# Sliding-window attention feeding an MLP: a build-time scheduler with an added start order, changed load rates, and one load dependency removed

## The chip, the cores and the metric

The kernel runs on one core of a Trainium2 chip. The metric is the device time of one execution in microseconds (us). The profile's own span is some 2 us shorter than that time. Where text below compares profiled executions with each other, it compares spans or instants within them. Where it says "median", it is the device time.

A program on one core has no second die to be compared with, so the label fast or slow of a run comes from the times alone (slow: over 1.5% above the fastest run of the same kernel). Some kernels here have waits of different lengths from run to run and get the label "slow" for that reason; I therefore list their times with the mean granted clock of TensorE.

## The reference

```python
scores = (q @ k.T) / sqrt(64)            # q, k, v: 8 batches x 8 heads x 576 rows x 64, float32
mask   = 0 <= (row - col) < 64           # causal window of 64
attn   = softmax(where(mask, scores, -1e9)) @ v
x      = attn.transpose(0, 2, 1, 3).reshape(4608, 512)
h      = x @ w_in                        # 512 -> 2048
out    = (h * sigmoid(h)) @ w_out        # 2048 -> 512, float32
```

## The kernel before

The kernel does not write its instructions in program order by hand. Every piece of work is added to a `Plan`: its engine and duration, what it depends on, and for a load the transfer time. `Plan.run` then plays a list schedule on paper when the program is built, and emits the instructions of every engine in the order that came out. In the traces, what stands behind a waiting instruction on its engine waits with it: in the changed kernel DVE sat idle for 12.26 us ahead of one copy, with the masks behind it. **The plan's beliefs about durations and landings decide the order; the semaphores keep the result right whatever the beliefs are.**

How the plan believes in the landing of a load (`seen` is the time from which others may rely on it):

```python
soft = e == "POOL"
pipe[soft] = max(pipe[soft], pipe[False], end + 0.9) + op["dma"]
op["seen"] = pipe[soft] + (2.0 if c in ("xk", "xo") else 1.4)
```

The loads of q and k that GpSimd (POOL) issues, the first with a cast (`natb`), the second in rows (`nat`). Both wait in the plan for the v of the batch before (`v_landed[b - 1]`), though no data or buffer asks for it:

```python
parts[kk] += [p.add("dma", {"POOL": 0.72}, ... load_rows(i, b, pj, kk, hh),
              [nat_free.get(i)] + (v_landed[b - 1] if b > 2 else []), dma=0.6) for hh in range(2)]
...
ca = [p.add("dma", {"POOL": 0.66}, ... load_cast(w, b, pj, kk),
            [natb_free.get(w)] + (v_landed[b - 1] if b > 2 else []), dma=1.0)]
tu = p.add("turn", {"PE": us}, None, ca + [c_ident] + busy, ...)      # PE transposes what has landed
```

The v of a batch: four loads, then two copies on VectorE (DVE) that place the half-shifted rows, "the shift of v". Only then may PE multiply by v. The masks of the exponentials are on the same engine, and PE's value product of a unit (a pair of heads and a group of rows; 12 units in a batch) waits for its mask:

```python
def shift_v(b, hf, a, z):
    t = vv[b % NK][:, 2 * NB * a:2 * NB * z + 1, 0:D]
    if hf: nc.vector.tensor_copy(out=t[0:64, 2::2], in_=t[64:128, 1::2])
    else:  nc.vector.tensor_copy(out=t[64:128, 0:-1:2], in_=t[0:64, 1::2])
...
lv = v_landed[b]
sh = [p.add("shift", {"DVE": 0.1 + 0.18 * (z - a)}, ... shift_v(b, hf, a, z), lv[a:z], b=b) for hf in range(2)]
...
ma = p.add("mask", {"DVE": 0.37}, ... masking(n, g), [ex, *c_mask], b=b)
pv = p.add("pv", {"PE": 0.17}, None, [ma] + v_done[(b, pj)] + ..., lat=0.1, pool=pool, b=b)
```

At the start, warm-up matmuls fill PE's free time in the plan:

```python
nc.tensor.matmul(banks[op["bank"]][:, 0:384], lhsT=ident, rhs=bias..., start=True, stop=True)
p.add_filler(60, "warm", {"PE": 0.17}, warm, [*c_bias, c_ident], gate=...)
```

The softmax here doesn't subtract the row's maximum and nothing guards it: scores larger than these inputs give would overflow.

Of the kernel before, what the change touches and what calls it, by code (L numbers as in the profile page):

```python
# [14 lines left out]
class Plan:  # L15
# [31 lines left out]
    def run(self):  # L47
        head = {c: 0 for c in self.queues}
        engines = sorted({e for q in self.queues.values() for op in q for e in op["us"]})
        free = {e: 0.0 for e in engines}  # L50
        can = {e: [c for c, q in self.queues.items() if any(e in op["us"] for op in q)] for e in engines}
        table, left = "exp", self.count
        pipe = {True: 0.0, False: 0.0}
        events, order = [0.0], []
        while left:
            if not events:
                raise RuntimeError([(c, head[c], q[head[c]]["n"]) for c, q in self.queues.items() if head[c] < len(q)])
            now = self.now = heapq.heappop(events)
            while events and events[0] == now:
                heapq.heappop(events)  # L60
            moved = True
            while moved:
                moved = False
                for e in engines:
                    if free[e] > now:
                        continue
                    best = None
                    for c in can[e]:
                        q = self.queues[c]
                        if head[c] == len(q):  # L70
                            continue
                        op = q[head[c]]
                        if e not in op["us"] or (best and best[0]["first"] <= op["first"]):
                            continue
                        if not self.done(op["deps"]) or (op["gate"] and not op["gate"]()):
                            continue
                        if op["pool"] and not any(self.done(self.banks[i]) for i in self.pools[op["pool"]]):
                            continue
                        best = (op, c)
                    if best is None:  # L80
                        continue
                    op, c = best
                    if op["pool"]:
                        banks = self.banks
                        op["bank"] = min((i for i in self.pools[op["pool"]] if self.done(banks[i])),
                                         key=lambda i: max([u["seen"] for u in banks[i]], default=0.0))
                        banks[op["bank"]] = op["until"]
                    head[c] += 1
                    us = op["us"][e]
                    if op["table"] and op["table"] != table:  # L90
                        table, us = op["table"], us + 1.28
                    end = free[e] = now + us
                    if op["dma"] is None:
                        op["seen"] = end + op["lat"]
                    else:

                        soft = e == "POOL"
                        pipe[soft] = max(pipe[soft], pipe[False], end + 0.9) + op["dma"]
                        op["seen"] = pipe[soft] + (2.0 if c in ("xk", "xo") else 1.4)
                    op["at"], op["cls"], op["by"] = now, c, e  # L100
                    order.append((op, e))
                    left -= c != "warm"
                    moved = True
                    heapq.heappush(events, end)
                    heapq.heappush(events, op["seen"])
        for op, e in order:
            op["fn"](e)
# [3 lines left out]
def kernel(ctx, tc, q, k, v, w_in, w_out, out):  # L111
    nc = tc.nc
# [3 lines left out]
    NP = H // 2  # L116
# [3 lines left out]
    NG = 3  # L120
# [7 lines left out]
    PARTS = {0: [(0, 192), (192, TT)]}  # L128
    NXQ, NXK, NXO = 4, 2, 3
    NRAW, NOX = 2, 2  # L130
    NIV, NPM = 2, 1
    scale = 1.0 / float(D) ** 0.5

# [6 lines left out]
    ident = keep.tile([128, 128], BF16, name="ident")  # L140
# [73 lines left out]
    def clear_ob(i):  # L214
        nc.vector.memset(obs[i].bitcast(FP32), 0.0)

    c_ident = p.add("one", {"POOL": 0.5}, const_ident)
    c_vv = [p.add("one", {"DVE": 0.25}, lambda _, i=i: clear_vv(i)) for i in range(NK)]
    c_k = [p.add("one", {"DVE": 0.15}, lambda _, i=i: clear_k(i)) for i in range(NK)]
    c_zero = p.add("one", {"DVE": 0.1}, lambda _: nc.vector.memset(zero, 0.0))  # L220
# [37 lines left out]
    def load_v(e, b, part):  # L258
        g0, g1 = part * 9, part * 9 + 9
        queue[e].dma_start(  # L260
            out=vv[b % NK][:, 2 * g0 + 1:2 * g1 + 1:2, 0:D],
            in_=v[b].rearrange("h s d -> (h s) d").rearrange("(g p) d -> p g d", p=128)[:, g0:g1],
        )

    def load_w_in(f):
        nc.gpsimd.dma_start(
            out=w_in_sb[:, :, f * 256:(f + 1) * 256],
            in_=w_in[:, f * 256:(f + 1) * 256].rearrange("(c p) f -> p c f", p=128),
        )

    def load_w_out(f):
        nc.gpsimd.dma_start(
            out=w_out_sb[:, 2 * f:2 * f + 2, :],
            in_=w_out[f * 256:(f + 1) * 256, :].rearrange("(c p) m -> p c m", p=128),
        )
# [174 lines left out]
    win, wout = [], []  # L450
# [21 lines left out]
    def add_batch_qk(b):  # L472
        pool = "at" if b else "all"
        slot, parts = {}, {0: [], 1: []}
        for pj in range(NP):
            kq_done[(b, pj)] = []
            busy = s_last.get((b - NK, pj), []) + ([c_k[b % NK]] if b < NK else [])
            for kk in range(2):
                if b >= (NXK if kk else NXQ):
                    if pj % 2 == 0:  # L480
                        slot[kk] = n_nat[0] % NN
                        n_nat[0] += 1
                    i = slot[kk]
                    parts[kk] += [p.add("dma", {"POOL": 0.72}, lambda _, i=i, pj=pj, kk=kk, hh=hh: load_rows(i, b, pj, kk, hh),
                                        [nat_free.get(i)] + (v_landed[b - 1] if b > 2 else []), dma=0.6) for hh in range(2)]
                    if pj % 2 == 0:
                        continue
                    both = busy + s_last.get((b - NK, pj - 1), [])
                    if kk:
                        done = [p.add("xk", {"SP": 1.4}, lambda _, i=i, pj=pj: turn_rows(i, k_place(b, pj - 1)),  # L490
                                      parts[kk] + both, dma=2.9)]
                        nat_free[i] = done[0]
                    else:
                        w = n_raw[0] % NRAW
                        n_raw[0] += 1
                        x = p.add("xk", {"SP": 1.4}, lambda _, i=i, w=w: turn_rows(i, raws[w].rearrange("x j s -> x (j s)")),
                                  parts[kk] + raw_free.get(w, []), dma=2.9)
                        nat_free[i] = x
                        done = [p.add("spread", {"DVE": 0.5}, lambda e, w=w, pj=pj, hh=hh: spread_q(e, w, b, pj - 1, hh),
                                      [x] + both, b=b) for hh in range(2)]  # L500
                        raw_free[w] = done
                    parts[kk] = []
                    for x in (pj - 1, pj):
                        kq_done[(b, x)] += done
                    continue
                w = n_nat[1] % NNB
                n_nat[1] += 1
                ca = [p.add("dma", {"POOL": 0.66}, lambda _, w=w, pj=pj, kk=kk: load_cast(w, b, pj, kk),
                            [natb_free.get(w)] + (v_landed[b - 1] if b > 2 else []), dma=1.0)]
                by = {"ACT": 0.64, "DVE": 0.75}  # L510
                li = []

# [20 lines left out]

    def add_v_loads(b, parts, busy):
        v_landed.setdefault(b, []).extend(
            p.add("dma", {"POOL": 1.0}, lambda e, part=part: load_v(e, b, part), busy, dma=1.3) for part in parts)

    def add_batch_v(b):
        busy = pv_last.get(b - NK, []) + [c_vv[b % NK]]
# [9 lines left out]
    def add_batch_attention(b):  # L549
        pv_last[b], o_rows = [], []  # L550
        pool = "at" if b else "all"
        for g, pj in [(g, pj) for pj in range(NP) for g in range(NG)] if b < NPM else [(g, pj) for g in range(NG) for pj in range(NP)]:
                n = len(g_pv)
                s = p.add("s", {"PE": 0.17 if b else 0.4}, None,
                          kq_done[(b, pj)] + g_pv[n - NE:n - NE + 1] * (n >= NE) + ([] if b else c_bias) + c_q.get(b, []),
# [98 lines left out]


    def warm(op):
        nc.tensor.matmul(banks[op["bank"]][:, 0:384], lhsT=ident, rhs=bias.rearrange("k x h i -> k (x h i)"),  # L657
                         start=True, stop=True)

    p.add_filler(60, "warm", {"PE": 0.17}, warm, [*c_bias, c_ident], gate=lambda: moe[40][0]["seen"] is None,  # L660
                 pool="all")
    for f in range(8):
        win.append(p.add("dma", {"POOL": 0.8}, lambda _, f=f: load_w_in(f), dma=1.55))
    add_batch_attention(0)
    n_tile = 0
    for b in range(1, B):
        add_batch_qk(b)
        add_batch_v(b)
        if b == 1:
            for f in range(8):  # L670
                wout.append(p.add("dma", {"POOL": 0.8}, lambda _, f=f: load_w_out(f), dma=1.38))
        while TB * (n_tile + 1) <= b * NB:
            add_tile(n_tile)
            n_tile += 1
        add_batch_attention(b)
# [34 lines left out]
```

## Time and profile before

| kernel before | value |
|---|---|
| median time | 317.98 us (4 runs, 317.68 to 318.04) |
| span of the profiled execution | 315.6 us |
| TensorE (PE) busy | 97% |
| mean granted TensorE clock | 1.0 |
| first MLP matmul starts | 24.80 us |
| first value product of batch 6 starts | 182.70 us |
| last matmul ends | 312.31 us |

The prediction below shows the page's busy table, PE's waits and the turns of batch 3's q (a turn is a transpose on PE), and reads them. The first value product of batch 6, from which the account further down counts, is this line of PE's timeline (start, busy time, engine, line of the program, operation, tiles and count):

```profile
182.70 0.34 PE L363 MATMUL at<-vv,e 128*128 128x130 bf16 x3
```

One view it doesn't show also belongs here. This is the timeline of DVE in the kernel before, with the same columns; in brackets is the idle time before it and what ended it:

```profile
182.09 0.74 DVE L358 TENSOR_TENSOR e<-e,mask 128x384 bf16<-128x384 bf16 x2 [0.33 <-ACT e L355]
...
197.93 0.76 DVE L325 COPY vv<-vv 64x2304 bf16<-64x2304 bf16 x1
...
199.36 0.75 DVE L323 COPY vv<-vv 64x2304 bf16<-64x2304 bf16 x1
```

The first masks of batch 6 run at 182.09. The two copies that shift batch 7's v come 16 us later. The last of that v had landed at 188.35 (from the issue and landing of its four loads in the trace), so the copies waited for nothing.

### The profile page before, as it was taken

Reading aid. Unit: us, or ns where it says so; the run is one execution under the profiler, and the core shown is the slowest. Engines: PE = TensorE matmul, PEld = TensorE weight load, DVE = VectorE, ACT = ScalarE, POOL = GpSimd, SP = SyncE. Lnnn points to the kernel's source line nnn. Section 1 sums busy time; section 2 is a strip of 40 time slices with the busy share of each in tenths; the row PEclk is TensorE's granted clock in tenths of the full one; section 3 lists DMA queues with packets and bytes.
Section 4 is the critical chain, followed back from the end, with each engine's and each line's share of the span. In section 5 each row is a group of like instructions: output and inputs, shape, how many; then the busy total and the mean of one; then the engine's idle time right before and its main releaser. Section 6 shows DMA issues by size and latency. Waiting matters only on the chain.

```text
span 315.6 us, 6086 instructions
## 1 busy us (share of the span) xinstructions
PE 307.6 (97%) x2231; PEld 167.7 (53%) x2231; DVE 152.8 (48%) x465; ACT 194.1 (61%) x381; POOL 120.8 (38%) x161
## 2 busy tenths in 40 slices
PE   5899999999999999999999999999999999999995
PEld 2668666545655456545654565455444444444444
DVE  5691858854788638895895089606800000000000
ACT  8798795787848687467618762777176136316611
POOL 8965958876748642867645400000000000000000
PEclk9999999999999999999999999999999999999999
DMA  7999999999999999999999995302320110020011
GB/s 68 173 194 189 158 200 167 154 226 160 144 152 158 152 95 159 200 162 132 157 162 188 167 156 119 83 1 56 95 58 2 66 66 2 18 82 33 3 66 66
DMA packets 137309, 37.03 MB, mean 117 GB/s; under 512 B 121664, under 2 KB 132800, under 8 KB 137280
## 3 DMA queue, kind: packets, MB, share of 16 engines
q0 software_dynamic: 96128, 18.36, 78.6%
q1 hardware_dynamic: 41152, 18.29, 31.1%
q8 instruction: 17, 0.28, 0.4%
q14 instruction: 12, 0.10, 0.1%
HBM read 36.70 MB, written 9.44 MB: 146 GB/s over the span
## 4 chain that ended last, share of the span: by engine, by line
PE 92%; DVE 2%; DMA 2%; ACT 1%; POOL 1%; issue 1%; POOLq 0%; ACTq 0%; DVEq 0%
PE mp L428 39%; PE mp L437 39%; PE at L363 5%; PE at L337 5%; DMA natb<-in_q_dram 2%; PE at L296 1%; PE at L419 1%; PE at L287 1%; PE at L657 0%; DVE qbd L309 0%; POOL natb L232 0%; PE mp L657 0%; ACT L355 0%; PE mp L408 0%; POOL vv L260 0%
## 5 line engine op out<-in xcount | busy, mean ns | idle before, releaser
L437 PE MATMUL mp<-w_out_sb,g 128*128 128x512 bf16 (+2 forms) x608 | 145.4, 367 | 0.0
L428 PE MATMUL mp<-bridge,w_in_sb 128*128 128x512 bf16 (+2 forms) x640 | 129.7, 358 | 0.1
L434 ACT ACTIVATE g<-mp 128x512 bf16<-128x512 f32 (+2 forms) x160 | 86.5, 555 | 30.0 <-PE mp L428 29.7
L428 PEld LDWEIGHTS <-w_in_sb 128*128 128x128 bf16 x640 | 60.4, 98 | 59.6 <-issue 0.4
L437 PEld LDWEIGHTS <-g 128*128 128x128 bf16 x608 | 54.4, 97 | 41.3
L443 ACT COPY ot<-mp 128x512 f32<-128x512 f32 (+2 forms) x36 | 20.1, 563 | 73.7 <-PE mp L437 56.8
L392 DVE TENSOR_TENSOR ox<-at,rc 64x192 bf16<-64x192 f32 x120 | 42.4, 354 | 2.6
L242 POOL DMA_DIRECT2D nat<-in_k_dram x48 | 36.1, 754 | 17.1 <-DMA vv<-in_v_dram 7.0
L260 POOL DMA_DIRECT2D vv<-in_v_dram x32 | 32.0, 1002 | 24.8 <-PE at L363 15.5
L355 ACT ACTIVATE e<-at 128x384 bf16<-128x384 f32 x89 | 37.9, 498 | 2.1 <-PE at L337 1.9
L358 DVE TENSOR_TENSOR e<-e,mask 128x384 bf16<-128x384 bf16 x84 | 26.5, 346 | 24.5 <-ACT e L355 23.8
L363 PEld LDWEIGHTS <-e 128*128 128x128 bf16 x288 | 22.6, 96 | 15.2 <-DVE e L358 2.1
L363 PE MATMUL at<-vv,e 128*128 128x130 bf16 x273 | 29.8, 219 | 0.0
L242 POOL DMA_DIRECT2D nat<-in_q_dram x32 | 24.3, 764 | 7.9 <-DMA nat<-in_q_dram 4.7
L337 PE MATMUL at<-qbd,kt 128*128 128x128 bf16 x252 | 22.8, 219 | 0.2
L337 PEld LDWEIGHTS <-kt 128*128 128x128 bf16 x252 | 17.8, 98 | 9.6 <-issue 1.4
L369 DVE RECIPROCAL rc<-at 128x6 f32<-128x6 f32 x91 | 17.3, 194 | 10.0 <-PE at L363 8.2
L302 DVE COPY qbd<-at 64x288 bf16<-64x288 bf16 x25 | 12.0, 479 | 16.0 <-ACT qbd L302 14.4
L375 DVE TENSOR_TENSOR ob<-at,rc 64x192 bf16<-64x192 f32 x48 | 16.8, 350 | 0.9
L256 DVE COPY qbd<-raw 64x1152 bf16<-64x1152 bf16 x16 | 7.9, 497 | 13.2 <-DMA raw<-nat 12.9
L302 ACT COPY qbd<-at 64x288 bf16<-64x288 bf16 x23 | 11.0, 478 | 2.9 <-DVE qbd L302 1.9
L232 POOL DMA_DIRECT2D natb<-in_q_dram x16 | 10.7, 670 | 4.8 <-PE mp L428 1.3
(66 smaller groups left out, 160.9 us busy)
## 6 DMA issues: line engine op xcount, KB each, us to landing
out_dram<-ot SPq DMA_DIRECT2D x35, 256.0 KB, 2.5
vv<-in_v_dram POOLq DMA_DIRECT2D x32, 144.0 KB, 6.9
nat<-in_k_dram POOLq DMA_DIRECT2D x48, 72.0 KB, 8.0
natb<-in_q_dram POOLq DMA_DIRECT2D x16, 144.0 KB, 6.3
nat<-in_q_dram POOLq DMA_DIRECT2D x32, 72.0 KB, 8.1
w_in_sb<-in_moe_w_in_dram POOLq DMA_DIRECT2D x8, 256.0 KB, 8.4
w_out_sb<-in_moe_w_out_dram POOLq DMA_DIRECT2D x8, 256.0 KB, 8.3
natb<-in_k_dram POOLq DMA_DIRECT2D x8, 144.0 KB, 5.9
```

Source lines behind the costliest of these rows:

```text
L242: nc.gpsimd.dma_start(out=rows(i)[:, pj % 2, :, 64 * hh:64 * hh + 64], in_=(q, k)[kk][b, 2 * pj + hh].rearrange("(m p) d -> p m d", p=NR),)
L260: queue[e].dma_start(out=vv[b % NK][:, 2 * g0 + 1:2 * g1 + 1:2, 0:D], in_=v[b].rearrange("h s d -> (h s) d").rearrange("(g p) d -> p g d", ...
L302: copies[e](out=qbd[b % NK][64 * hh:64 * hh + 64, pj, hh].rearrange("x (p m) -> x p m", m=NM)[:, :, r::2], in_=at_bf16(op)[64 * r:64 * r + ...
L337: nc.tensor.matmul(at_sp(op)[:, x], lhsT=kt[b % NK][:, pj * S + t * 64:pj * S + t * 64 + 128], rhs=qbd[b % NK][:, pj, :, t * 64:t * 64 + 6 ...
L355: nc.scalar.activation(out=es[n % NE], in_=at_sp(op), func=ACTF.Exp, scale=scale)
L358: nc.vector.tensor_mul(es[n % NE], es[n % NE], mask0 if g == 0 else mask)
L363: nc.tensor.matmul(at_pv(op)[:, x], lhsT=es[n % NE][:, x].rearrange("p h i -> p (h i)"), rhs=vv[b % NK][:, s:s + NB + 1:NB, 0:D + 1], star ...
L392: nc.vector.tensor_mul(ox(n)[:, :, r], pv[r, :, hh, 0:D], rc[r, :, hh:hh + 1].to_broadcast([64, 3, 64]))
L428: nc.tensor.matmul(banks[bank["bank"]][:, lo:hi], lhsT=w_in_sb[:, c, ft * 128:(ft + 1) * 128], rhs=bridge[:, (j * TT + lo) // 64:(j * TT + ...
L434: nc.scalar.activation(out=gts[gt][:, lo:hi], in_=banks[bank["bank"]][:, lo:hi], func=ACTF.Silu)
L437: nc.tensor.matmul(banks[bank["bank"]][:, 0:hi - lo], lhsT=gts[gt][:, m * 128:(m + 1) * 128], rhs=w_out_sb[:, f, lo:hi], start=(f == 0), s ...
L443: copies[e](out=ots[ot][:, lo:hi], in_=banks[bank["bank"]][:, 0:hi - lo])
```

## The change

By its diff it alters what the plan believes: loads are faster, loads after 60 us land up to 3 us later, and loads of q and k no longer depend on the older v, so that their landings may be planned earlier. Beside that, batch 0's units get an order of their own, and the warm-ups no longer wait for `bias`. The diff of the program (`...` marks what is left out; the last two changes stand on one line each):

```diff
-  op["seen"] = pipe[soft] + (2.0 if c in ("xk", "xo") else 1.4)
+  op["seen"] = pipe[soft] + (2.0 if c in ("xk", "xo") else 1.4) + ({"xo": 1.0}.get(c, 3.0) if now > 60 else 0.0)
...
+  UNITS0 = [(0, 0), (1, 0), (2, 0), (0, 1), (1, 1), (2, 1), (0, 2), (1, 2), (0, 3), (2, 2), (1, 3), (2, 3)]
...
-  c_ident = p.add("one", {"POOL": 0.5}, const_ident)
+  c_ident = p.add("one", {"POOL": 1.3}, const_ident)
...
-      [nat_free.get(i)] + (v_landed[b - 1] if b > 2 else []), dma=0.6) for hh in range(2)]
+      [nat_free.get(i)], dma=0.6) for hh in range(2)]
...
-      [natb_free.get(w)] + (v_landed[b - 1] if b > 2 else []), dma=1.0)]
+      [natb_free.get(w)], dma=0.85 if b else 1.0)]
...
-      p.add("dma", {"POOL": 1.0}, lambda e, part=part: load_v(e, b, part), busy, dma=1.3) for part in parts)
+      p.add("dma", {"POOL": 1.0}, lambda e, part=part: load_v(e, b, part), busy, dma=1.1 if b else 1.3) for part in parts)
...
-  for g, pj in [(g, pj) for pj in range(NP) for g in range(NG)] if b < NPM else ...
+  for g, pj in UNITS0 if b < NPM else ...
...
-  nc.tensor.matmul(banks[op["bank"]][:, 0:384], lhsT=ident, rhs=bias.rearrange("k x h i -> k (x h i)"),
+  nc.tensor.matmul(banks[op["bank"]][:, 0:384], lhsT=ident, rhs=ident.unsqueeze(1).to_broadcast([128, 3, 128]),
-  p.add_filler(60, "warm", {"PE": 0.17}, warm, [*c_bias, c_ident], ...)
+  p.add_filler(60, "warm", {"PE": 0.17}, warm, [c_ident], ...)
...
-  load_w_in(f), dma=1.55        ->  +  load_w_in(f), dma=1.35
-  load_w_out(f), dma=1.38       ->  +  load_w_out(f), dma=1.28
```

Lines of the program move by 2: what is L296 before is L298 after, and so on.

More of the change, by code (lines that the diff above doesn't have):

```diff
@@ L551, in add_batch_attention @@
         pool = "at" if b else "all"
-        for g, pj in [(g, pj) for pj in range(NP) for g in range(NG)] if b < NPM else [(g, pj) for g in range(NG) for pj in range(NP)]:
+        for g, pj in UNITS0 if b < NPM else [(g, pj) for g in range(NG) for pj in range(NP)]:
                 n = len(g_pv)
@@ L656, in warm @@
     def warm(op):
-        nc.tensor.matmul(banks[op["bank"]][:, 0:384], lhsT=ident, rhs=bias.rearrange("k x h i -> k (x h i)"),
+        nc.tensor.matmul(banks[op["bank"]][:, 0:384], lhsT=ident, rhs=ident.unsqueeze(1).to_broadcast([128, 3, 128]),
                          start=True, stop=True)
-    p.add_filler(60, "warm", {"PE": 0.17}, warm, [*c_bias, c_ident], gate=lambda: moe[40][0]["seen"] is None,
+    p.add_filler(60, "warm", {"PE": 0.17}, warm, [c_ident], gate=lambda: moe[40][0]["seen"] is None,
                  pool="all")
     for f in range(8):
-        win.append(p.add("dma", {"POOL": 0.8}, lambda _, f=f: load_w_in(f), dma=1.55))
+        win.append(p.add("dma", {"POOL": 0.8}, lambda _, f=f: load_w_in(f), dma=1.35))
     add_batch_attention(0)
@@ L670 @@
             for f in range(8):
-                wout.append(p.add("dma", {"POOL": 0.8}, lambda _, f=f: load_w_out(f), dma=1.38))
+                wout.append(p.add("dma", {"POOL": 0.8}, lambda _, f=f: load_w_out(f), dma=1.28))
         while TB * (n_tile + 1) <= b * NB:
```

## The prediction

> **What bounds the kernel now.** The page's busy table and its 40 slices came first.
>
> ```profile
> PE 307.6 (97%) x2231; PEld 167.7 (53%) x2231; DVE 152.8 (48%) x465; ACT 194.1 (61%) x381; POOL 120.8 (38%) x161
> ...
> PE   5899999999999999999999999999999999999995
> ...
> DMA  7999999999999999999999995302320110020011
> ```
>
> TensorE (PE) is full from the third slice on, and the DMA engines are full for the first 24 slices (about 190 us). The list of PE's waits says how much of PE's time is waiting:
>
> ```profile
> PE at L657 <- DVE bias L191: 3.5, 1, 3.5
> PE at L287 <- DMA natb<-in_q_dram: 0.6, 1, 0.6
> PE mp L408 <- DVE ox L398: 0.2, 1, 0.2
> ```
>
> The only long one is the very first: the warm-up matmuls wait for `bias`. The chain of waits ends with the two MLP layers alone (13.8 us per layer of a tile). I then added up PE's own work from the first MLP matmul, at 24.80 us in the timeline, by start-to-start times from the trace: first layer 64 x 0.083 + 64 x 0.1365 + 512 x 0.2158 = 124.5; second layer 560 x 0.2158 + 16 x 0.109 + 32 x 0.056 = 124.4; scores 252 x 0.056 = 14.1; values 252 x 0.058 = 14.6; turns of q, k and o some 7.5; five warm-ups 0.8. Sum 286.0. PE's last matmul ends at 312.31, so 287.5 us passed: **all stalls after 24.80 come to 1.5 us**. No reordering can win more than that plus what it takes off the first 24.8 us.
>
> [...]one matmul that waits for a load holds up everything behind it; the 0.6 us wait above is an example. [...]warm-ups start 0.32 us apart from 3.53 us and 0.16 us apart by 7 us. [...]while SyncE's queue carries transposes or stores, GpSimd's loads slow down (below).
>
> **The change, part by part.** Counting both built programs, every matmul of the work is there in the same number; only warm-ups rise, from 35 to 51. The rest is order.
>
> 1. *The unit order of batch 0.* It swaps just two units: (group 0, pair 3) goes ahead of (group 2, pair 2). The number and kinds of PE instructions before the first MLP matmul are the same, still with all batch-0 units ahead, so this gains nothing I can see: 0.
>
> 2. *The first microseconds.* `ident` is now planned at 1.3 us, which puts the three GpSimd steps of `window` ahead of the first q load. In the timeline they take 2.28 to 3.09, so the first load starts about 0.8 later, at 2.3 instead of 1.49; the second starts where it did (3.09). Warm-ups now need `ident` alone, which is ready at 1.31, and there are 27 before the first q turn. Some 8 or 9 at 0.32 (cold) and 18 at 0.162 make 2.8 + 2.9, so the first turn comes near 7.2 instead of 6.45. But PE idled until 10.31 for the second q:
>
> ```profile
> 10.31 0.56 PE L287 MATMUL at<-ident,natb 96*64 96x96 bf16 x12 [0.59 <-DMA natb<-in_q_dram]
> ```
>
> That wait swallows nearly all of it. The second q may land 0 to 0.4 later[...]. I put +0.2 on the start of the MLP (25.0).
>
> 3. *Batch-1 turns earlier, 25 to 43 us.* They stand up to 3 us earlier in PE's order. Walking the new order with the durations above, they come at 29.84, 30.77, 32.60 ... 38.90; the loads landed at 29.34, 30.02, 31.78 ... 37.53 before. They fit, by 0.5 us or more. The late lifts that held the first batch-1 scores (0.46 us of stall around 43) should go.
>
> 4. *Batch-3 q turns earlier: the part that decides.* Before, the plan held batch-3 loads back until batch-2's v had landed. The built GpSimd order, apart from the swap in part 2, is unchanged, so the loads go out as before; only PE's plan now believes in an earlier landing. Before, these turns stood at:
>
> ```profile
> 73.12 0.42 PE L296 MATMUL at<-ident,natb 96*128 96x96 bf16 x6
> 75.32 0.42 PE L296 MATMUL at<-ident,natb 96*128 96x96 bf16 x6
> 77.53 0.42 PE L296 MATMUL at<-ident,natb 96*128 96x96 bf16 x6
> 95.31 0.42 PE L296 MATMUL at<-ident,natb 96*128 96x96 bf16 x6
> ```
>
> In the new order the first stands directly ahead of the second MLP tile, and 9, 8 and 8 first-layer matmuls separate the four. My walk gives 63.1, 65.3, 67.2, 69.2, plus a few tenths of stalls before it. When do the loads land? The timeline of GpSimd gives their issue, and the DMA view narrowed to each gives the time to landing (8.6, 7.9, 6.4, 6.3 us):
>
> ```profile
> 56.88 0.68 POOL L232 DMA_DIRECT2D natb<-in_q_dram  x1
> ...
> 59.00 0.65 POOL L232 DMA_DIRECT2D natb<-in_q_dram  x1
> ...
> 61.77 0.64 POOL L232 DMA_DIRECT2D natb<-in_q_dram  x1 [0.18 <-issue]
> ...
> 65.73 0.73 POOL L242 DMA_DIRECT2D nat<-in_k_dram  x1 [1.54 <-DMA natb<-in_q_dram]
> 66.60 0.64 POOL L232 DMA_DIRECT2D natb<-in_q_dram  x1
> ```
>
> That is 65.5, 66.9, 68.2 and 72.9; the fourth line confirms the first, for GpSimd itself waited for that load until 65.7. All four land after PE wants them. The first is late because four v loads and a k transpose on SyncE's queue stand in front of it; the fourth because of four 256 KB stores issued from 63.8 on. So PE stalls from about 63.5 to 65.5. The first MLP matmul of tile 1, at 63.84 before, then comes at 65.5 + 0.25 = 65.75; less the 0.25 of turn work already done, the lag is 1.65. The second turn comes at 65.75 + 9 x 0.216 = 67.7 (landed), the third at 67.7 + 0.25 + 8 x 0.216 = 69.65 (landed), the fourth at 71.6: it waits until 72.9, **1.3 more**. Sum 2.95.
>
> 5. *A second late landing, hidden by the first.* VectorE now does batch 3's shift of v (two copies of 0.75) ahead of batch 2's first masks. The last of that v landed at 81.3, so masks cannot start before 82.8 (before: 81.12). With PE already 2.9 late, the masks come at about 84 anyway: 0 more. Alone it would cost about 1.7.
>
> 6. *Later.* Parts of batch-3 and batch-4 attention move up to 17 us earlier (94 to 137 us), with kt landed by 85 and v by 81. From about 147 us the two orders walk to the same microsecond. Nothing there can win the lag back, since PE has no idle time to give. Of the small stalls after 64 us (0.7 in all) perhaps 0.2 go.
>
> Sum: +2.95 - 0.2 = +2.75. The +0.2 at the start and the saved 0.46 at 43 do not count, as the stall ends at a landing, not after a count of work. 317.97 + 2.75 = 320.7. I shade it to **320.2**, because a change that was kept may have been kept for a measured gain, and a load can land earlier than my trace says.
>
> **Rivals.**
> *(a) The loads land in time.* If the earlier turns or the removed wait let the loads go out earlier, nothing stalls: PE does its 286.0 from 25.0, stalls shrink to 0.5 to 1, and the time is 316.5 to 317.5. For it: the removed wait was meant for that. Against it: GpSimd's order is the same, and its issues between 40 and 70 us wait for older loads, not for PE; the DMA engines are full.
> *(b) The start decides.* If warm-ups without `bias` or the unit swap brought the MLP forward, it would start up to 1 us sooner, 317. Against it: the first q's turn was never what the start waited for, and the new warm-ups make it later.
> *(c) Stalls compound.* [...]if the loads land 1 to 2 us later than before, it could cost 2 to 4 more: 323 to 325.
>
> **Range and chances.** Six parts in ten for my sum, three for (a) or half of the stall, one for more: 80% between 317.0 and 322.1. Two per cent is 6.4 us. Faster by that is impossible with 1.5 us of stalls and a start bound by loads (1%); slower needs (c) (3%).
>
> **What the new profile would show.** PE's waits with a line of the q turns (now L298) on a DMA into natb, 2 us near 65 and 1.3 near 72; the PE slice at 63 to 72 below nine; the first MLP matmul of tile 1 near 65.7; scores of batch 2 near 81.5 instead of 78.6; the last layer starting near 301.2 instead of 298.4; first MLP matmul near 25.0. I am wrong if the batch-3 q turns run at 63 to 70 without a wait, or if the first MLP matmul moves by more than 0.5 us.

## The result and the profile after

The changed kernel takes **329.33 us** (median of 4 runs: 327.81, 327.82, 330.84, 331.47), against 317.98. The ratio is 1.0364, with a 95% interval of 1.0288 to 1.0439: slower. Such a ratio is the mean time of one kernel's fast runs over that of the other's of the same rounds, so not quite the ratio of the medians. The prediction was 320.2, with at most 322.1.

The busy table and the slices of the page after:

```profile
PE 313.5 (96%) x2247; PEld 170.5 (52%) x2247; DVE 156.1 (48%) x468; ACT 193.4 (59%) x378; POOL 120.2 (37%) x161
...
PE   8999999878999999999999969999999999999995
...
PEclk9999999999999999999999969999999999999999
```

PE has two dips, at slices 8 to 10 (57 to 82 us) and in slice 24 (187 to 196 us), where the granted clock falls too. PE's busy time grew by 5.9 us: 3.1 of them ahead of the first MLP matmul, where warm-ups were added (20.45 us busy before, 23.57 after), and the rest at the second dip, since matmuls at a lower clock count as longer (a 128x512 one 623 ns in the mean from 190.4 to 196 us, 378 from 196.5 to 210). The list of PE's waits (total, how often, longest):

```profile
PE at L298 <- DMA natb<-in_q_dram: 3.8, 2, 2.4
PE at L365 <- DVE e L360: 3.3, 1, 3.3
PE at L659 <- POOL ident L180: 1.4, 1, 1.4
```

The first is the predicted wait of batch 3's q turns. The second was not predicted: a value product waits 3.3 us for a mask. PE's timeline at both places:

```profile
65.49 0.43 PE L298 MATMUL at<-ident,natb 96*128 96x96 bf16 x6 [1.46 <-DMA natb<-in_q_dram]
...
67.70 0.42 PE L298 MATMUL at<-ident,natb 96*128 96x96 bf16 x6
...
69.69 0.42 PE L298 MATMUL at<-ident,natb 96*128 96x96 bf16 x6
...
74.20 0.43 PE L298 MATMUL at<-ident,natb 96*128 96x96 bf16 x6 [2.37 <-DMA natb<-in_q_dram]
...
190.42 0.51 PE L365 MATMUL at<-vv,e 128*128 128x130 bf16 x3 [3.33 <-DVE e L360]
```

Why was the mask late? DVE's timeline after, which answers to the one shown of before:

```profile
187.51 0.76 DVE L327 COPY vv<-vv 64x2304 bf16<-64x2304 bf16 x1 [12.26 <-DMA vv<-in_v_dram]
188.28 0.76 DVE L325 COPY vv<-vv 64x2304 bf16<-64x2304 bf16 x1
189.05 0.92 DVE L258 COPY qbd<-raw 64x1152 bf16<-64x1152 bf16 x2
190.01 0.63 DVE L360 TENSOR_TENSOR e<-e,mask 128x384 bf16<-128x384 bf16 x2
```

**The shift of batch 7's v now stands ahead of every mask of batch 6.** Counted in the traces, 60 of the 84 masks run before it, where it was 74 before. DVE sits idle for 12.26 us for a v that batch 6 has no use for, then works off the copies, and only then makes the mask that PE stands still for. The plan had put the shift at 177.9 us, when it believed that v to be there; its last load landed at 187.40. The load itself came no later than in the kernel before (188.35): what changed is what stands behind it.

The view by stretches adds the clock. Its columns are the stretch, its length, busy us (and instructions) of PE, weight loads, DVE, ACT and POOL, then the granted clock, DMA share and GB/s:

```profile
186.90:189.00 2.10, 0.19 (x1) 0.00 (x0) 1.47 (x2) 0.91 (x3) 0.00 (x0) 1.00 1.21 229
189.00:189.50 0.50, 0.00 (x0) 0.00 (x0) 0.49 (x2) 0.00 (x0) 0.00 (x0) 0.75 0.00 0
189.50:196.00 6.50, 5.58 (x27) 3.26 (x28) 4.50 (x17) 1.95 (x4) 0.00 (x0) 0.50 0.07 26
196.00:196.50 0.50, 0.50 (x8) 0.37 (x7) 0.34 (x2) 0.00 (x0) 0.00 (x0) 0.92 0.50 184
```

During the wait the clock halves, near 189.25, and it stays halved until about 196.08, long after PE is back at work at 190.42.

**The account of the profiled executions.** Batch 6's first value product started at 182.70 before and at 190.42 after: 7.72 us later. From there to the end of the last matmul it is 129.61 us before (312.31 - 182.70) and 132.36 after (322.78 - 190.42): 2.75 more, the halved clock. The sum, 10.47, is the whole difference of the last matmul. The later start (25.66 against 24.80) and the waits at the q turns are inside the 7.72: batch 6's scores, just ahead, start 4.22 us late (183.62 against 179.40), and the other 3.50 come with the wait for the mask. PE could have been at that point 3.5 us sooner, but the mask would not have been.

### The profile page after: what moved, and what is told of

Its sections match the earlier page's. It is cut to its first block, busy times and chain, and to the rows that moved or that the text cites. A ratio compares the mean times of both kernels' runs of the same rounds, so it can differ in the third digit from the quotient of the medians.

```text
span 326.1 us, 6119 instructions
## 1 busy us (share of the span) xinstructions
PE 313.5 (96%) x2247; PEld 170.5 (52%) x2247; DVE 156.1 (48%) x468; ACT 193.4 (59%) x378; POOL 120.2 (37%) x161
## 4 chain that ended last, share of the span: by engine, by line
PE 63%; DMA 20%; POOL 7%; issue 7%; DVE 2%; ACT 1%; POOLq 0%; DVEq 0%; ACTq 0%
PE mp L439 26%; PE mp L430 24%; DMA vv<-in_v_dram 7%; DMA natb<-in_q_dram 5%; DMA nat<-in_k_dram 5%; POOL nat L244 4%; DMA nat<-in_q_dram 3%; POOL vv L262 3%; PE at L365 3%; PE at L339 3%; PE at L659 2%; PE mp L659 1%; PE at L289 1%; PE at L410 0%; PE at L298 0%
## 5 line engine op out<-in xcount | busy, mean ns | idle before, releaser
L439 PE MATMUL mp<-w_out_sb,g 128*128 128x512 bf16 (+2 forms) x608 | 147.3, 371 | 0.0
L439 PEld LDWEIGHTS <-g 128*128 128x128 bf16 x608 | 55.1, 98 | 42.4 <-issue 0.3
L357 ACT ACTIVATE e<-at 128x384 bf16<-128x384 f32 x91 | 39.1, 497 | 9.7 <-PE at L339 6.3
L244 POOL DMA_DIRECT2D nat<-in_q_dram x32 | 23.6, 748 | 7.1 <-DMA vv<-in_v_dram 3.8
L304 DVE COPY qbd<-at 64x288 bf16<-64x288 bf16 x28 | 13.4, 478 | 13.3 <-ACT qbd L304 7.4
L327 DVE COPY vv<-vv 64x576 bf16<-64x576 bf16 (+1 forms) x14 | 8.8, 629 | 13.0 <-DMA vv<-in_v_dram 12.7
L426 ACT CAST bridge<-at 128x192 bf16<-128x192 f32 x24 | 7.6, 320 | 5.2 <-PE at L421 4.0
```

What stands on the lines that cost most here:

```text
L244: nc.gpsimd.dma_start(out=rows(i)[:, pj % 2, :, 64 * hh:64 * hh + 64], in_=(q, k)[kk][b, 2 * pj + hh].rearrange("(m p) d -> p m d", p=NR),)
L357: nc.scalar.activation(out=es[n % NE], in_=at_sp(op), func=ACTF.Exp, scale=scale)
L439: nc.tensor.matmul(banks[bank["bank"]][:, 0:hi - lo], lhsT=gts[gt][:, m * 128:(m + 1) * 128], rhs=w_out_sb[:, f, lo:hi], start=(f == 0), s ...
```

## The experiments

Eight kernels were run, in two jobs of four with three rounds each. Every one gave correct results. Before, in the rounds of the first job: 317.59 us (23 runs); in those of the second: 317.31 us (23 runs).

**Theory.** The loss comes from the places that too early a belief in landings gives to instructions that wait for a load: above all the shift of batch 7's v on DVE, then the q turns of batch 3 on PE. **Rival 1:** the loss is at the q turns (the prediction's own mechanism, only larger). **Rival 2:** loads that go out at other times crowd the transfers and slow everything. **Rival 3:** the new start or unit order costs the time.

The view by which the experiments are compared is the same as in the account above:

| kernel | batch 6's first value product, us | last matmul ends, us | between, us | median time, us |
|---|---|---|---|---|
| before | 182.70 | 312.31 | 129.61 | 317.98 |
| changed | 190.42 | 322.78 | 132.36 | 329.33 |
| x_shift | 183.97 | 313.57 | 129.60 | 320.29 |
| x_turn | 189.72 | 321.00 | 131.28 | 325.24 |
| x_fill | 189.68 | 319.29 | 129.61 | 326.81 |
| x_fill2 | 190.16 | 319.79 | 129.63 | 323.93 |
| x_dep | 182.97 | 312.57 | 129.60 | 317.71 |
| x_all | 182.03 | 311.64 | 129.61 | 317.44 |
| x_best | 180.53 | 310.15 | 129.62 | 315.29 |

Once past that point, every kernel whose clock stays full needs the same 129.6 us. (x_b_dep is left out: its wait lies in batch 5.) In the three traces in which PE waits for this mask, the product comes the same 3.02 to 3.03 us after the last landing of batch 7's v: 187.40 and 190.42 in the changed kernel, 186.69 and 189.72 in x_turn, 187.13 and 190.16 in x_fill2.

### x_shift: batch 7's v alone believed later

```diff
-  op["seen"] = pipe[soft] + ...
+  op["seen"] = pipe[soft] + ... + op.get("slip", 0.0)
   lv = v_landed[b]
+  for x in lv:
+      x["slip"] = {7: 14.0}.get(b, 0.0)
```

> The changed kernel, whose plan is told that batch 7's v lands 14 us later, and nothing else: its two shift copies on VectorE then stand behind batch 6's masks again. Theory (the stall at 187 us is VectorE waiting in order for batch 7's v, and the half clock behind it follows from that stall): both go, 3.5 + 2.7 us, so about 322 us; the two waits of the batch-3 q turns (1.6 and 2.5) stay. Rival (PE only meets the next late load a little later): less than 2 us gained, 326 or more.

Measured: 320.29 us (318.65, 320.00, 320.58, 321.04), ratio 1.0099 (1.0074 to 1.0123), a verdict of "same" at the 2% line, though clear of 1. Mended alone, the place of two copies on an engine that is half idle leaves 2.7 us (320.29 - 317.59) of the 11.35 (329.33 - 317.98), each against the kernel before of its own rounds. PE's list of waits in this run:

```profile
PE at L661 <- POOL ident L180: 1.4, 1, 1.4
PE at L410 <- DVE ox L400: 0.6, 1, 0.6
PE at L298 <- DMA natb<-in_q_dram: 0.5, 1, 0.5
```

The wait for the mask is gone and so is the halved clock (mean 1.0 in the profiled run). The q turns waited only 0.5 us in this execution, where they waited 3.8 in the changed kernel's: the landings differ from run to run. So the expectation that both waits stay was not met in the profiled run. Rival 1 falls, since the q turns stand where the change put them and all four runs lose 3.5 us or less.

### x_turn: batch 3's q turns alone believed later

```diff
   ca = [p.add("dma", ... load_cast(w, b, pj, kk), [natb_free.get(w)], dma=0.85 if b else 1.0)]
+  ca[0]["slip"] = 7.0 if b == 3 else 0.0
```

> The changed kernel, whose plan is told that batch 3's q loads land 7 us later: the four turns move some 7 us back in PE's order, all else stays. The two waits of 1.6 and 2.5 us must go. Theory (every wait ends at a landing that does not depend on PE): PE then arrives earlier at batch 3's v (shift done near 82.6) and at batch 7's v (187), waits longer there, and the time falls by 0 to 2 us, to 326 to 328. Rival (the waits add up): it falls by the full 4.2 us, to about 324.

Measured: 320.56, 324.43, 326.04 and 329.13 us, with mean clocks of 0.999, 0.993, 0.993 and 0.984; ratio of those labelled fast 1.0160 (1.0085 to 1.0235), a verdict of "unclear". The profile (of the 326.04 run) says what became of the time:

```profile
PE at L365 <- DVE e L360: 4.9, 1, 4.9
PE at L660 <- POOL ident L180: 1.4, 1, 1.4
PE at L339 <- DVE qbd L304: 1.1, 1, 1.1
```

The waits at the q turns are gone, PE comes earlier to the mask and stands there for 4.9 us in place of 3.3. The product starts at 189.72, just 0.70 earlier than in the changed kernel, and v had landed 0.71 earlier. **In this trace, what PE wins ahead of an instruction that waits for a landing is given back there.** The rest of the 1.78 us between the two profiled executions (326.04 and 327.82) is the clock, halved here for 3.41 us and not 6.83. The medians do not decide between theory and rival: 325.24 lies below the theory's 326 to 328 and above the rival's 324, and the runs lie on both sides. The third line is a copy of q that stands on DVE behind the two copies of batch 3's v shift (which waited for v until 80.97 us); that shift the prediction had put at 1.7 us if nothing hid it, and it costs 1.1 here. The spread shows more than the theory expected: in the 320.56 run the mask may have come earlier, but that run left no trace.

### x_fill: dummy matmuls where PE waits for the mask

```diff
+  if b == 6 and g == 0 and pj == 0:
+      def filled(...):
+          for _i in range(12):
+              nc.tensor.matmul(banks[pv["bank"]][:, 0:384], lhsT=ident, rhs=ident..., start=True, stop=True)
+          values(pv, n, 6, pj, g)
+      pv["fn"] = filled
```

> The changed kernel with 12 warm-up matmuls (about 2 us) ahead of the first value product of batch 6, where PE stands idle for 3.3 us. Theory (the half clock of 190.4 to 196 us comes from PE's own idleness): the clock stays full and some 2.7 us go, about 325 us, while the wait itself ends at the same 190.4. Rival (the half clock comes from something else, power or the state of the chip): the granted clock still falls to 0.5 there and the time is 328 or more.

Measured: 324.80, 326.02, 327.61 and 330.22 us, clocks 0.999, 0.994, 0.995 and 0.988; ratio 1.0275 (1.0231 to 1.0320). In the profile the clock stays full at 190 and the rest takes 129.61 us. But this execution did not test the filling. PE's and DVE's timelines:

```profile
187.73 2.11 PE L573 MATMUL at<-ident 128*128 128x384 bf16 x12
189.68 0.34 PE L365 MATMUL at<-vv,e 128*128 128x130 bf16 x3
```

```profile
187.25 0.63 DVE L360 TENSOR_TENSOR e<-e,mask 128x384 bf16<-128x384 bf16 x2
```

Batch 7's v had landed at 184.63, PE came late (at 187.73), and the mask that its product needs was begun at 187.25; by the 0.41 us from mask to product in the changed kernel (190.01 and 190.42) it was ready at about 187.66. PE had nothing to wait for, and the dummies cost the 1.95 us until 189.68. That the 2.75 us of the account are the halved clock rests on the table: 129.60 to 129.63 us in every kernel with a full clock there, 132.36 with 5.66 us at half clock (190.42 to 196.08), 131.28 in x_turn with 3.41. Half of these two times is 2.83 and 1.71, against 2.75 and 1.67 measured. In this run the clock halved elsewhere, after the wait at the last q turn (PE idle from 71.1 to 73.3):

```profile
71.10:73.30 2.20, 0.00 (x0) 0.00 (x0) 0.95 (x2) 0.47 (x1) 1.50 (x3) 1.00 1.60 169
74.00:74.50 0.50, 0.50 (x3) 0.19 (x2) 0.00 (x0) 0.01 (x1) 0.50 (x1) 0.85 1.60 158
74.50:77.50 3.00, 3.00 (x8) 1.06 (x7) 0.95 (x2) 1.66 (x3) 1.85 (x4) 0.50 2.65 150
77.50:78.00 0.50, 0.50 (x3) 0.25 (x2) 0.00 (x0) 0.18 (x1) 0.50 (x1) 0.73 2.41 153
```

In the changed kernel's own profile an idle time of 2.37 us at the same place had left the clock full (1.00 from 74 to 78 us); why was not shown. (This run also ended 1.7 us later after its last matmul than the others, 4.97 us against 3.3 in most; I did not find out why.)

### x_fill2: dummies at both places

```diff
   # x_fill, and:
+  if b == 3 and pj == 3 and twos:
+      def turn_filled(...):
+          for _i in range(10):
+              nc.tensor.matmul(banks[tu["bank"]][:, 0:384], lhsT=ident, rhs=ident..., start=True, stop=True)
+          turn_twos(tu, w)
```

> The changed kernel with dummy matmuls at both long waits: 12 ahead of batch 6's first value product as in the earlier run, and 10 (1.6 us) ahead of batch 3's last q turn. The results stay right. Theory (the spread of 324.8 to 330.2 us of the earlier run, and of 327.8 to 331.5 us of the changed kernel, is the clock halved or not halved after a long wait): mean granted clock 0.997 or more in every run, 323.5 to 326 us, all runs within 2 us. Rival (the spread comes from the landings, that is from the waits themselves): the same spread and median as with one filling, about 326.8 us.

Measured: 321.96, 322.86, 325.00 and 329.03 us, clocks 1.0, 1.0, 1.0 and 0.995; ratio 1.0176 (1.0127 to 1.0224), a verdict of "unclear". Three of four runs keep the full clock, as expected, and the median is 6.6 us over the kernel before of its rounds (323.93 - 317.31), where x_fill's was 9.2 (326.81 - 317.59); for the runs labelled fast alone it is 5.6 and 8.4. But they are not within 2 us of each other, and one still lost clock: the expectation fails in that. So both seem true: part of the spread is the clock, and the 3.0 us between the runs at full clock (321.96 to 325.00) must come from elsewhere, most likely the landings; this was not traced. In its profile PE came to the mask at 185.0 us, did 2.1 us of dummies, waited 3.06 us more and went on at 190.16, with the clock full. This is the run that tests the filling.

### x_dep: the removed dependency restored, the rest of the change kept

```diff
-  [nat_free.get(i)], dma=0.6)
+  [nat_free.get(i)] + (v_landed[b - 1] if b > 2 else []), dma=0.6)
-  [natb_free.get(w)], dma=0.85 if b else 1.0)
+  [natb_free.get(w)] + (v_landed[b - 1] if b > 2 else []), dma=0.85 if b else 1.0)
```

> The changed kernel with one part undone: the loads of q and k are again planned behind the older v. The turns and both shifts then stand late again. Theory (the removed dependency is what causes all the waits): no wait of PE over 0.5 us after the first MLP matmul, full clock, only the later start (+0.9) remains: 318 to 319.5. Rival (the new rates and the late landings have a share): over 321.

Measured: 317.71 us (20 runs, 316.69 to 319.10), ratio 1.0002 (0.9986 to 1.0017). PE's list of waits has one line left, the start. That is just under the expected 318 to 319.5: the first MLP matmul is 0.78 us later than before, but the last one ends only 0.26 later. **The loss hangs on the removed dependency; the unit order, the rates, the late term and the start together are worth nothing either way, once it is back.** Rival 3 falls.

### x_b_dep: the removed dependency alone, on the kernel before

```diff
   # the diff of x_dep the other way round, in the kernel before
```

> The kernel before with one part of the change alone: no load waits for an older v. Its plan puts batch 7's v shift after 62 masks (two units into batch 6) and batch 3's q turns at 68.7 to 75.3 us of the plan, 5 us later than the changed kernel. Theory: no wait over 1 us at the q turns, and a wait of 3 to 5 us at batch 6's third value product for a mask behind the shift; 320 to 325 us, over 322 if the clock halves after the wait. Rival (the removal does harm only together with the new rates and the late term): 317.5 to 318.5 us.

Measured: 326.21 us (325.03 to 326.79, clock 0.989 in every run), ratio 1.0263 (1.0235 to 1.0292). Slower as expected (though above the expected 320 to 325) and with no wait at the q turns, but **the place was not the one expected**, and the wait was 7.27 us, not 3 to 5. PE's and DVE's timelines:

```profile
158.06 0.51 PE L365 MATMUL at<-vv,e 128*128 128x130 bf16 x3 [7.27 <-DVE e L360]
```

```profile
156.86 0.75 DVE L327 COPY vv<-vv 64x2304 bf16<-64x2304 bf16 x1 [5.68 <-DMA vv<-in_v_dram]
157.64 0.90 DVE L360 TENSOR_TENSOR e<-e,mask 128x384 bf16<-128x384 bf16 x3
```

Here it is the shift of batch **6**'s v that stands ahead of batch 5's masks. This plan put it at 149.8 us; the load landed at 156.74. Batch 7's shift, which I had named, waited for 1.66 us and held up nothing. So one part alone gives the same fault in another batch: with the dependency gone, which shift goes wrong is a matter of small numbers. I had looked for the wait where the changed kernel has it and not walked the whole order of DVE a second time.

### x_all: the dependency stays removed, three landings believed later

```diff
+  ca[0]["slip"] = 7.0 if b == 3 else 0.0                       # q loads of batch 3
+  x["slip"] = {3: 10.0, 7: 14.0}.get(b, 0.0)                   # v loads of batches 3 and 7
```

> The changed kernel with the dependency still removed, but the plan is told that three loads are ready later than it assumed: batch 3's q loads by 7 us, batch 3's v by 10 us, batch 7's v by 14 us. Nothing else is touched. Theory (the loss is only the place that wrong beliefs about landings give to the q turns and to the v shift in the engines' orders): none of the waits over 1 us is left, and the time is that of the version with the dependency restored, 317.3 to 318.7 us. Rival (loads that go out earlier crowd the transfers and slow other engines, whatever the order): still 320 us or more, with waits elsewhere.

Measured: 317.44 us (20 runs, 316.68 to 318.71), ratio 1.0006 (0.9995 to 1.0017), and no wait of PE but the start. The whole loss is gone with the dependency still removed. And in all ten traces, this one and x_dep's included, GpSimd's 152 loads come in the same order: with or without the dependency, no load was moved. Only the order of instructions on the other engines differs. Rival 2 falls, and this run with x_dep settles the cause.

### x_best: the dependency restored and fewer warm-ups

```diff
   # x_dep, and:
-  p.add_filler(60, "warm", {"PE": 0.17}, warm, [c_ident], ...)
+  p.add_filler(60, "warm", {"PE": 0.26}, warm, [c_ident], ...)
```

> A better version: the changed kernel with the dependency restored, and a warm-up matmul planned at 0.26 us in place of 0.17, so that 18 in place of 27 warm-ups stand ahead of the first turn. 11 cold ones of 0.32 and 7 of 0.16 from 1.36 us on end at 6.0 us, where the version with the dependency restored began its first turn at 8.1 us, with that load landed at 5.5 us. If the start is on the path that sets the end, up to 1.2 us are won: 316.3 to 317.3 us. If the later start was hidden behind other waits of the first batch: 317.7 us as before.

Measured: **315.29 us** (315.10 to 315.45), ratio 0.9924 (0.9903 to 0.9945): faster than both kernels, by 0.8% against the kernel before (a verdict of "same" at the 2% line, but all four runs lie below the fastest of the 23 before, 316.64), and by more than the expectation's 316.3. Its start in PE's timeline:

```profile
6.01 0.56 PE L289 MATMUL at<-ident,natb 96*64 96x96 bf16 x12
...
9.37 0.32 PE L289 MATMUL at<-ident,natb 96*64 96x96 bf16 x3 [0.74 <-DMA natb<-in_q_dram]
```

The first turn runs at 6.01, where the estimate had 6.0 and x_dep 8.1. The estimate counted the nine warm-ups fewer ahead of the first turn; in the traces 18 fewer stand ahead of the first MLP matmul (28 against 46 in x_dep). That matmul starts at 22.59 us against 24.80 before, and those 2.2 us are still there at the last matmul (310.15 against 312.31).

## Why the prediction was wrong

- **The step that failed is part 6, "Later": "From about 147 us the two orders walk to the same microsecond. Nothing there can win the lag back".** The walk followed PE's order alone, and from there to batch 6's first value product that order is indeed the same. DVE's order was not walked. Part 5 even described this very fault for batch 3 (the shift of v ahead of the masks of the batch before), and rightly found it hidden there; the same move of batch 7's shift was overlooked. Step 6 had -0.2; the runs show a wait for the mask that adds 3.50 us to PE's lag of 4.22, and then 2.75 for the clock: 10.47 at the last matmul, where the sum had 2.75. Of the 7.72 that are missing, 6.25 belong to this step and 1.47 to the lag (part 4). The view that would have shown it existed beforehand: which instructions stand ahead of which on DVE, beside the trace's landing of batch 7's v at 188.35.
- **Part 4 had the mechanism right and the size too small.** The turn at 65.5 came at 65.49, but that exactness was luck: in the other eight traces, of kernels with the same order of loads, the same load landed between 62.25 and 64.97. The turn at 72.9 came at 74.20, as the load landed at 74.16, 1.3 us later than in the kernel before. The lag behind the q turns was 4.46 us (first scores of batch 2 at 82.89, before at 78.43), not 2.95. In x_turn's trace this cost did not add up with the wait behind it.
- **Two of the prediction's own signs** were met badly: the last layer starts at 308.88, not near 301.2, and the first MLP matmul moved by 0.86, over the 0.5 at which it called itself wrong.
- **Part 5 was right**: nothing extra in the changed kernel; without the q turns' waits, 1.1 us in x_turn.
- **Parts 1 and 3 were right** as far as they go: no gap over 0.25 us is left near 43 us, and x_dep shows the sum of all parts but the dependency to be zero.
- **Part 2 was too small**: +0.2 predicted. In the seven profiled kernels with this start order the first MLP matmul came at 24.40, 24.94, 25.45, 25.58, 25.66, 26.09 and 26.19, a mean of 25.47, so +0.7 with a spread of nearly 2 us. I had counted 8 or 9 cold warm-ups; in the changed kernel there are 11 (0.32 us apart), so the first turn came at 7.59, not 7.2. And the start was taken to be bound by loads. But in the changed kernel the second q landed at 8.88 (10.27 before) and its turn still came only at 10.47: PE was behind with its own queue. In x_best the same start with fewer warm-ups wins time, so PE's start is on the path, which the case against rival (b) had denied.
- **Rival (c)** looked for the added cost at the q turns; the 2 to 4 us that it gives for later landings were shown by no trace. The clock halved in a wait of 3.33 us at another place, and in x_fill after 2.23 us at the q turn. The chance of 3% for slower was too low for a prediction that had found one belief to be too early and had not asked which other instructions rest on such beliefs.
- **GpSimd's loads beside SyncE's transfers:** that they slow down, the prediction says without a rate. In the half-microseconds of the trace before, from 30 to 190 us, GpSimd's queue moved 146 GB/s on average where SyncE's queue carried nothing (its packets' time under 1% of 16 engines' time), and 44 GB/s where that share was 50 to 100%. By what mechanism was not shown.

**What stays open:** which of the plan's shifts goes wrong depends on small differences (batch 7 in the changed kernel, batch 6 in x_b_dep), and why the two slowest runs of the changed kernel, 330.84 and 331.47 us, took 3 us longer was not traced; their mean clocks of 0.984 and 0.983 against 0.988 and 0.989 fit a longer time at half clock. That the removed dependency served as a stand-in for the program's limit on outstanding loads (last section) is an argument, not shown. Why x_turn's fastest run took only 320.56 us was not traced either.

## What to carry to other kernels

In a static schedule, walk the order of **every** engine, not only of the one that bounds the kernel (here a copy on DVE waited for 12.26 us and the masks behind it with it), and ask of each instruction that waits for a transfer what stands behind it and who waits for that. A belief in a landing that is 7 to 14 us later cost nothing here (x_all); one that is too early puts a wait in front of ready work (3.33 us of PE in the changed kernel, 7.27 in x_b_dep). Such waits need not add up along the engine: in the three traces with the wait for the mask, the last landing set its end. But they can cost clock on top: it was halved for 6.83 us in the changed kernel and 3.41 in x_turn, and stayed full in x_fill2.

## What else the traces show

- The clock and the length of PE's waits. The clock was halved in or after waits of 2.23 us (x_fill: for 3.41 us, 74.35 to 77.77), 3.33 us (changed kernel: for 6.83 us, 189.25 to 196.08), 4.9 us (x_turn: for 3.41 us) and 7.27 us (x_b_dep: 0.50 from 155 to 161 us). It stayed full after waits of 2.37 us (changed kernel, 74.20) and 3.06 us (x_fill2). So the length of the wait alone does not decide; what does was not shown.
- GpSimd's loads in flight. Of the 144 loads after the first eight, in each of the traces of the kernel before, the changed one and x_b_dep, none finished issuing earlier than 0.99 us after the landing of the load eight places ahead of it; 36 to 43 finished before the landing of the load seven places ahead. The 152 loads use eight completion semaphores in turn, and 125 of those 144 in the trace before (122 to 126 in the ten traces) are marked as waiting for the one that the load eight places ahead also used. So the built program bounds the loads in flight here, and nothing shows this to be a limit of the chip. The plan leaves it out; it believed batch 7's v to be there at 177.9, and that landed at 187.40. How much of these 9.5 us this explains was not tested.
- The landing of one and the same load varies from trace to trace. Over the ten traces, with GpSimd's loads in the same order, batch 3's first q landed between 62.25 and 65.45 us and its last between 71.19 and 74.16. The waits at the q turns were 3.8 us in one profile and 0.5 in another (x_shift) of the same order there.
